# The first feature groups of a fused recurrence and two-layer network, taken unit by unit

## The chip, the cores and the metric

The kernel runs on one core of one Trainium2 chip. The metric is the time of one execution on the device, in microseconds (us). Engines: TensorE (PE, with its weight loads as PEld), VectorE (DVE), ScalarE (ACT), GpSimd (POOL) and SyncE (SP), which issues most DMAs; POOL issues the weights' loads.

## The reference

Four sequences of 768 steps with 8 heads of 48 dimensions go through a linear recurrence, and its output (3072 tokens of 384) through two networks:

```python
for t in range(S):
    cur = einsum('bhd,bhe->bhde', u * k[t], v[t])
    y[t] = einsum('bhd,bhde->bhe', r[t], state + cur)
    state = w[t][:, :, :, None] * state + einsum('bhd,bhe->bhde', k[t], v[t])
x = y.transpose(0, 2, 1, 3).reshape(B * S, H * D)
x = ((x @ w_a) * (x @ w_b)) @ w_out
h = x @ w_in
out = (maximum(h, 0) + alpha * minimum(h, 0)) @ w_out2
```

The first network has 1536 features, the second 2048. All data are float32.

## The kernel before, in words

**Products.** Each float32 operand of a large product is split in two: a high part (rounded to the type float32r) and a low part, the rest. A product is then three: high by high, low by high, high by low (`gemm3`, nine matmuls over three slices of 128, and `out1`, `out2` for the second factor). ACT makes the high part and DVE the low part.

**The recurrence.** It is cut into 12 units of 256 tokens. A unit has two forms of its inputs: `T` (transposed r, k, w; 112 partitions) and `N` (natural r, k, w). On `N`, DVE computes products of near pairs of steps (`natural`), which go through DRAM (`diag`: one store `mb`, eight loads into the diagonal blocks of the mask matrix `M`). On `T`, DVE runs a tree over distances 1 to 32 (`tree`); before each tree step at or above the unit's sub-block size, PE multiplies the far pairs (`level`, PSUM tile `psl`) and ACT copies them into `M` (`extract`; in unit 1 DVE does it for the second head of each pair). Then come the transposes of k (`ktrans`, `psk`, copied to `kn`), the state products (`dstate`, `psd`), the state (`state`) and the output (`yout`, `psx`), which ACT and DVE split into the high and low part of x. Each pair of units is a block of 512 tokens.

**The first network.** `mlp1` runs once per block over 12 groups of 128 features (`f`). A group has two products `pa` and `pb` (nine matmuls of 512 columns each), ACT's copy `ca` of pa, DVE's product `mul`, the split into `g`, and nine matmuls into three accumulators `acc`. At the block's end ACT copies the three results (`cp`), and POOL stores them to DRAM (`x2d`). The second network, `mlp2`, follows for all six blocks.

**Weights.** `load_w` brings each 128 x 384 weight as 64-bit floats and converts it: `sign`, `expo` and `low` on ACT, `join` on DVE, `hi` on ACT, `lo` on DVE. The order in block 0 is a, b, out of group 0, then of group 1, and so on. The loads stand on POOL; each load but the first six waits, through a small copy `tick`, for the weight six places earlier. All 36 weights of the first network stay in tiles of one pool (`w`, 37 tiles of 3072 bytes per partition); A0, N1 and V1 of the first units borrow five of them at the start.

**Pools.** PSUM has three pools that matter here: `psacc` (three banks: the accumulators, and at the start the levels of units 0 and 1), `psatt` (three banks: everything else of the recurrence) and `psh` (two banks: pa and pb). A tile of a pool is given out in the order in which tasks were added, except in `ws` and `psacc`, where whoever is ready takes one. `T` is a pool of one tile, so the next unit's T can be loaded when all readers of the last one are done. T of unit 1 has a tile of its own.

**The order of the work.** Nothing is scheduled by hand. The class `Tasks` (line 35) collects tasks with an engine, an estimated duration, a priority (lower goes first), the names they read and write, and a pool. `run` (line 94) plays them through: each engine takes the ready task with the lowest priority number. The instructions are then written out in the order found, so each engine's queue is fixed before the kernel runs. Between 4.5 us and the start of the first pa (planner's time), PE gets filler matmuls on the identity (`warm`) where it is idle or its recent work is thin.

```python
bank(lev):  "acc", "psacc"  if u < len(BLOCKS[0]) and lev  else  "att", "psatt"
NW = 37;  WL = 6;  pools: ws 3, x2 2, T 1, psatt 3, psh 2, psacc 3
K.fill += [first_pa[0], 2900]
```

Of the kernel before, what the change touches and what calls it, by code (L numbers as in the profile page):

```python
# [22 lines left out]
CH = 128  # L23
# [11 lines left out]
class Tasks:  # L35
# [58 lines left out]
    def run(self):  # L94
# [51 lines left out]

        while left:
            progress = True
            while progress:
                progress = False  # L150
                for eng, q in ready.items():
# [3 lines left out]
                    for k, (p, i) in enumerate(q):  # L155
                        if at[i] > now + 1e-9:
                            continue
                        if eng == "PE" and warming() and low(now + t[i][1], self.work.get(i, 0.0)):
                            filler()
                            progress = True  # L160
                            break
# [22 lines left out]
                        heapq.heappush(ev, (end, serial, i))  # L184
                        progress = True
# [6 lines left out]
            if i >= 0:  # L192
                left -= 1
                for h in users.get(i, ()):
# [17 lines left out]
def rwkv_then_moe_kernel(  # L212
# [53 lines left out]
    W = {}  # L266
    prev = []
    WL = int(6)

    def load_w(key, src, pr, after=()):  # L270
        behind = None
        prev.append(key)
        gate = len(prev) == 1
        if gate:
            after = list(after) + ["m1/d2"]
        if len(prev) > WL:
            behind = prev[-1 - WL]
            after = list(after) + [f"w{behind[0]}{behind[1]}"]
        nm = f"w{key[0]}{key[1]}"
        raw, ws = nm + "r", nm + "s"  # L280
        c = {}

        def ld():
            c["raw"] = wp.tile([128, 384, 2], U32, tag="w", name="raw", bufs=NW)
            if gate:
                nc.gpsimd.tensor_copy(tick, first_m[1][96:97, 0, 0, 32:33])
            if behind:

                nc.gpsimd.tensor_copy(tick, W[behind][0:1, 0, 0:1].bitcast(F32))
            nc.gpsimd.dma_start(out=c["raw"].bitcast(I64).rearrange("p n one -> p (n one)"), in_=src)  # L290

        def sign():

            c["s"] = xp.tile([128, 384], U32, tag="ws", name="ws", bufs=3)
            nc.scalar.activation(  # L295
                out=c["s"].bitcast(F16).rearrange("p (n b) -> p n b", b=2)[:, :, 1], in_=c["raw"][:, :, 1].bitcast(F32),
                func=ACTF.Copy, scale=2.0 ** -100)

        def low():

            nc.scalar.activation(
                out=c["s"].bitcast(U16).rearrange("p (n b) -> p n b", b=2)[:, :, 0], in_=c["raw"][:, :, 0],
                func=ACTF.Copy, scale=7.49 * 2.0 ** -32)

        def expo():
            h = c["raw"][:, :, 1].bitcast(F32)
            nc.scalar.activation(out=h, in_=h, func=ACTF.Copy, scale=2.0 ** -112)

        def join():
            nc.vector.scalar_tensor_tensor(  # L310
                out=c["s"], in0=c["raw"][:, :, 1], scalar=3, in1=c["s"],
                op0=ALU.logical_shift_left, op1=ALU.bitwise_or)

        def hi():
            W[key] = wp.tile([128, 2, 384], F32R, tag="w", name="w", bufs=NW)
            nc.scalar.copy(W[key][:, 0], c["s"].bitcast(F32))  # L316

        def lo():
            tt(W[key][:, 1], c["s"].bitcast(F32), W[key][:, 0].bitcast(F32), ALU.subtract)

        add("Pool", 1.1, pr - 40, ld, r=after, w=[raw], alloc=("w", raw), nbytes=128 * 3072)
        yield
        add("ACT", act(384), pr, sign, r=[raw], w=[ws, raw + "/h"], alloc=("ws", ws))
        add("ACT", act(384), pr, expo, r=[raw], w=[raw + "/h"])
        add("ACT", act(384), pr, low, r=[raw, ws], w=[ws])
        add("DVE", dve(384), pr, join, r=[raw + "/h", ws], w=[ws])
        add("ACT", act(384), pr, hi, r=[ws], w=[nm], alloc=("w", nm))
        add("DVE", dve(384), pr, lo, r=[ws, nm], w=[nm + "/l"])


# [5 lines left out]
    def unit(u, pr):  # L336
# [3 lines left out]
        T, V = f"T{u}", f"V{u}" if u != 1 else "V1/x"  # L340

        N = {y: f"N{u}/{y}" if u != 1 else f"N1{y}/x" for y in "rkw"}
# [11 lines left out]
        def bank(lev):  # L354

            if u < len(BLOCKS[0]) and lev:
# [17 lines left out]
        def zn(cc, hd, k):  # L374
            return f"Z{cc}{hd}{k}" if u else f"z{cc}{hd}/{k}"
# [29 lines left out]
        def new_t():  # L405
            cur["T", u] = ap_.tile([112, 3, 8, CH], F32, tag="T", name="T")
# [5 lines left out]
        if u != 1:  # L412
            add("HOST", 0, p0, new_t, w=[f"{T}/new"], alloc=("T", T))
# [365 lines left out]
    def mlp1(j, pr, xnames, us):  # L779
# [7 lines left out]
        def out1(f, ks, ms=(0, 1, 2)):  # L787
            if f == 0 and ks[0] == 0:
                c["acc"] = [pp.tile([128, n], F32, tag="acc", name=f"acc{m}", bufs=3) for m in range(3)]
            order = [(i, m) for i in ks for m in ms]  # L790
            for i, m in order:
                wi, gi = ((0, 0), (1, 0), (0, 1))[i]
                mm(c["acc"][m], W["o", f][:, wi, 128 * m:128 * m + 128], c["g", f][:, gi],
                   f == 0 and i == 0, f == F1 - 1 and i == 2)

        def add_out(f, p):
            g, wo = f"g{j}_{f}", f"wo{f}"
            if f == 0:
                for m in range(3):
                    add("PE", 0, p, lambda: None, r=[g + "/h"], w=[f"{acc}_{m}"], alloc=("psacc", f"{acc}_{m}"))  # L800
            if f == F1 - 1:
                for m in range(3):
                    add("PE", 3 * MM, p, lambda m=m: out1(f, (0, 1, 2), (m,)), r=[g + "/h", g + "/l", wo, wo + "/l"],
                        w=[f"{acc}_{m}"])
# [374 lines left out]
```

## Time and profile before

| | us |
|---|---|
| three runs | 1004.85, 1007.99, 1011.61 |
| median | 1007.99 |
| profiled execution, own time | 1009.12 |
| its span (first to last instruction) | 1007.3 |
| mean granted TensorE clock | 0.993 of full speed |

The busy times in the profile's rows are those of the one profiled execution, counted from the start of its span. A clock of 1.00 is TensorE's level of 2.4 GHz, 0.50 the one of 1.2 GHz; values between are means over a stretch. In a timeline row the bracket at the end gives the idle time of the engine before the first instruction and what ended it.

### The profile page before, as it was taken

What the parts mean: (1) busy time and instruction counts of PE and PEld (TensorE: products, weight loads), DVE (VectorE), ACT (ScalarE), POOL (GpSimd) and SP (SyncE); (2) the same over time, 40 slices, a digit from 0 to 9 for tenths busy, and PEclk for the clock granted to TensorE, in tenths of its full rate; (3) what the DMA queues carried; (4) which work ended last, traced back from release to release, by engine and by line L of the source; (5) the groups of instructions that cost most, each with busy time, mean ns of one, the idle gap of its engine ahead of it and who ended that gap; (6) DMA issues with size and microseconds to landing.
All of it is one profiled execution on the core that took longest, in us unless ns stands there. A gap on an engine that the chain in (4) does not pass through costs nothing.

```text
span 1007.3 us, 21086 instructions
## 1 busy us (share of the span) xinstructions
PE 978.8 (97%) x8800; PEld 823.5 (82%) x8800; DVE 728.4 (72%) x1215; ACT 431.3 (43%) x931; POOL 87.7 (9%) x173
## 2 busy tenths in 40 slices
PE   6899999999999999999999999999999999999998
PEld 3558787877788878878788888898989898999998
DVE  8979899899999979897935668555554645554643
ACT  0796987535444363534438994121211121211111
POOL 1324120100100010000004331000000000000000
PEclk9999999999999999999999999999999999999999
DMA  7895563324141441415116551010100100000000
GB/s 215 211 242 167 180 165 105 107 71 129 50 132 44 116 138 41 127 41 155 18 43 206 172 171 64 1 32 32 32 32 1 32 32 1 32 1 1 32 1 32
DMA packets 78158, 85.61 MB, mean 85 GB/s; under 512 B 55600, under 2 KB 64944, under 8 KB 76784
## 3 DMA queue, kind: packets, MB, share of 16 engines
q1 hardware_dynamic: 70896, 52.81, 19.7%
q0 software_dynamic: 7168, 31.46, 9.9%
q8 instruction: 69, 1.13, 0.5%
q14 instruction: 25, 0.20, 0.1%
HBM read 73.24 MB, written 11.01 MB: 84 GB/s over the span
## 4 chain that ended last, share of the span: by engine, by line
PE 61%; DVE 20%; DMA 8%; ACT 7%; issue 3%; SPq 1%; DVEq 0%; ACTq 0%
PE acd L768 15%; PE hb L768 15%; PE hp L768 10%; PE pb L768 6%; DMA T<-in_rkw_t_dram 6%; PE pa L768 6%; PE acc L768 6%; DVE T L257 5%; DVE e L257 4%; DVE A L483 4%; PE psl L564 2%; DVE a L257 2%; DVE N L257 2%; DVE g L257 2%; ACT ws L295 1%
## 5 line engine op out<-in xcount | busy, mean ns | idle before, releaser
L768 PE MATMUL acd<-w,g 128*128 128x384 f32 x864 | 192.6, 335 | 0.0
L950 ACT CAST g<-g 128x512 fp32r<-128x512 f32 x96 | 59.6, 621 | 281.7 <-PE hb L768 173.1
L768 PE MATMUL acc<-g,w 128*128 128x512 f32 x648 | 174.7, 399 | 1.1 <-ACT g L830 1.1
L768 PE MATMUL pa<-x,w 128*128 128x512 f32 x648 | 162.0, 395 | 0.6 <-ACT a L819 0.3
L768 PE MATMUL pb<-x,w 128*128 128x512 f32 x648 | 159.8, 391 | 0.6 <-ACT w L316 0.5
L768 PEld LDWEIGHTS acd<-w,g 128*128 128x128 f32 x864 | 154.2, 188 | 1.8
L768 PEld LDWEIGHTS pa<-x,w 128*128 128x128 f32 x648 | 121.7, 189 | 27.8 <-ACT x L719 1.1
L768 PEld LDWEIGHTS pb<-x,w 128*128 128x128 f32 x648 | 121.2, 188 | 27.0 <-ACT w L316 0.9
L768 PEld LDWEIGHTS acc<-g,w 128*128 128x128 f32 x648 | 118.7, 189 | 26.3 <-ACT g L830 1.7
L257 DVE TENSOR_TENSOR T<-T 112x1024 f32<-112x1024 f32 (+4 forms) x144 | 116.4, 809 | 20.8 <-DMA T<-in_rkw_t_dram 17.2
L257 DVE TENSOR_TENSOR g<-g,g 128x512 fp32r<-128x512 f32 x96 | 66.2, 690 | 81.9 <-ACT g L950 81.3
L768 PE MATMUL hp<-x,w 128*128 128x512 f32 x432 | 103.0, 391 | 0.0
L830 ACT CAST g<-a 128x512 fp32r<-128x512 f32 x72 | 44.4, 617 | 135.8 <-DVE a L257 134.5
L768 PE MATMUL hb<-x,w 128*128 128x512 f32 x432 | 102.0, 389 | 0.0
L768 PEld LDWEIGHTS hb<-x,w 128*128 128x128 f32 x432 | 81.1, 188 | 16.8
L768 PEld LDWEIGHTS hp<-x,w 128*128 128x128 f32 x432 | 80.8, 188 | 16.0
L768 PE MATMUL hb<-w,g 128*128 128x384 f32 x288 | 92.5, 335 | 0.0
L483 DVE TENSOR_REDUCE A<-e 128x16 f32<-128x768 f32 (+15 forms) x148 | 85.9, 580 | 2.0
L941 DVE TENSOR_SCALAR g<-hp,al 128x512 f32<-128x512 f32 x48 | 36.0, 751 | 63.0 <-PE hp L768 63.0
L257 DVE TENSOR_TENSOR a<-a,pb 128x512 f32<-128x512 f32 x72 | 49.1, 682 | 19.3 <-PE pb L768 18.5
L564 PEld LDWEIGHTS psl<-T 48*16 48x16 f32 (+4 forms) x2432 | 39.6, 107 | 23.0 <-issue 12.7
L819 ACT COPY a<-pa 128x512 f32<-128x512 f32 x72 | 41.9, 581 | 31.6 <-PE pa L768 31.2
(76 smaller groups left out, 1095.4 us busy)
## 6 DMA issues: line engine op xcount, KB each, us to landing
raw<-in_wt_dram POOLq DMA_DIRECT2D x68, 384.0 KB, 4.0
T<-in_rkw_t_dram SPq DMA_DIRECT2D x36, 448.0 KB, 6.3
N<-in_rkw_n_dram SPq DMA_DIRECT2D x10, 1152.0 KB, 8.3
x2d<-x POOLq DMA_DIRECT2D x36, 128.0 KB, 2.1
x2r<-x2d SPq DMA_DIRECT2D x36, 128.0 KB, 2.2
out_dram<-o SPq DMA_DIRECT2D x24, 192.0 KB, 1.9
V<-in_v_s_dram SPq DMA_DIRECT2D x11, 384.0 KB, 7.1
Z<-in_v_s_dram SPq DMA_DIRECT2D x44, 96.0 KB, 3.0
```

The source lines that it names most:

```text
L257: nc.vector.tensor_tensor(out=out, in0=a, in1=b, op=op)
L295: nc.scalar.activation(out=c["s"].bitcast(F16).rearrange("p (n b) -> p n b", b=2)[:, :, 1], in_=c["raw"][:, :, 1].bitcast(F32), func=ACTF. ...
L483: nc.vector.tensor_reduce(out=v[:, :, d:d + (n - 1) * (SUB + 1) + 1:SUB + 1], in_=part(st["e"], 0, n), axis=AX.X, op=ALU.add)
L564: nc.tensor.matmul(out=st["ps"][o0:o0 + ms, cc, q, zc * i:zc * i + zc], lhsT=t[b0:b0 + 48, 1, q0 + q, t0:t0 + ms], rhs=r[b0:b0 + 48, q0 + ...
L768: nc.tensor.matmul(out=out, lhsT=lhsT, rhs=rhs, start=start, stop=stop)
L819: nc.scalar.copy(c["a", f], c["pa"])
L830: nc.scalar.copy(c["g", f][:, 0], c["a", f])
L941: nc.vector.tensor_scalar(out=st["m", f], in0=st["h", f], scalar1=0.0, scalar2=al[:, f:f + 1], op0=ALU.min, op1=ALU.mult)
L950: nc.scalar.copy(st["g", f][:, 0], st["m", f])
```

## The change

In block 0 the first three feature groups are computed for each unit apart: first with the 256 columns of unit 0, all three groups, then with those of unit 1. pa and pb of such a half share one PSUM tile, `hx`, with pa in the first 256 columns and pb in the others. From the fourth group on all is as before, and the fillers end with that group's pa. So that the accumulators can be taken early, only unit 0's levels use `psacc`; those of unit 1 go to `psatt`. Weights are loaded and converted two at a time, in 19 tiles of twice the size, three pairs ahead; a pair's conversion is the same six operations with 768 columns. T is one lasting tile `Tp`, whose parts r, k and w are tracked by name from unit to unit. The tiles borrowed at the start are three larger ones; two of unit 0's four Z tiles move into the one of A0. The copies `x2` of a block's result use the `ws` tiles (in the last block, M). In the planner's first 75 us, ACT and DVE stay free for up to 0.5 us where a task of clearly lower priority number is about to become ready (`soon`).

```diff
+        ends = {}
+
+        def soon(eng, p, dur):
+            c, at_ = {}, {}
+            for i, end in ends.items():
+                for s in succ[i]:
+                    if t[s][0] == eng and t[s][2] < p - 4.0:
+                        c[s] = c.get(s, 0) + 1
+                        at_[s] = max(at_.get(s, 0.0), end + (self.LAT[t[i][0]] if t[i][0] != eng else self.SAME.get(eng, 0.0)))
+            return any(c[s] == need[s] and at_[s] < now + min(0.5, dur) for s in c)
...
+                        if now < 75.0 and eng in ("ACT", "DVE") and soon(eng, p, t[i][1]):
                             break
...
+    Tp = ap_.tile([112, 3, 8, CH], F32, name="Tp")
...
-    NW = 37
+    NW = 19
-    for tag, n in (("w", NW), ("ws", 3), ("x2", 2), ("x", 2), ("a", 2), ("g2", 2), ("psatt", 3), ("psh", 2), ("psacc", 3),
-                   ("e", 1), ("kn", 1), ("T", 1), ("N", 1), ("V", 1)):
+    for tag, n in (("w", NW), ("ws", 2), ("x", 2), ("a", 2), ("g2", 2), ("psatt", 3), ("psh", 2), ("psacc", 3),
+                   ("e", 1), ("kn", 1), ("N", 1), ("V", 1)):
...
-    WL = int(6)
+    WL = int(3)
...
-            c["raw"] = wp.tile([128, 384, 2], U32, tag="w", name="raw", bufs=NW)
+            c["raw"] = wp.tile([128, 2, 384, 2], U32, tag="w", name="raw", bufs=NW)
...
+            if i >= WL:
+                nc.gpsimd.tensor_copy(tick, W[prev[i - WL][0]][0:1, 0, 0:1].bitcast(F32))
+            nc.gpsimd.dma_start(out=c["raw"].bitcast(I64).rearrange("p x n one -> p x (n one)"),
+                                in_=src.rearrange("x p n -> p x n"))
...
+        add("Pool", 1.1, pr - 40, ld, r=after, w=[R], alloc=("w", R), nbytes=128 * 6144)
         yield
+        add("ACT", act(768), pr, sign, r=[R], w=[S_, R + "/h"], alloc=("ws", S_))
+        add("ACT", act(768), pr, expo, r=[R], w=[R + "/h"])
+        add("ACT", act(768), pr, low, r=[R, S_], w=[S_])
+        add("DVE", dve(768), pr, join, r=[R + "/h", S_], w=[S_])
+        add("ACT", act(768), pr, hi, r=[S_], w=[nm + "/h"], alloc=("w", nm))
+        add("DVE", dve(768), pr, lo, r=[S_, nm + "/h"], w=[nm + "/l"])
...
-        T, V = f"T{u}", f"V{u}" if u != 1 else "V1/x"
+        T, V = "T1" if u == 1 else "Tp", f"V{u}" if u != 1 else "N1b/v"
...
-            if u < len(BLOCKS[0]) and lev:
+            if u == 0 and lev:
                 return "acc", "psacc"
             return "att", "psatt"
...
-    def mlp1(j, pr, xnames, us):
+    def mlp1(j, pr, xnames, us, pre=0):
...
+            def product(k, i):
+                if h is None:
+                    c[k, f, h] = pp.tile([128, n], F32, tag="h", name="p" + k, bufs=2)
+                else:
+                    if "hx" not in c:
+                        c["hx"] = pp.tile([128, 512], F32, tag="h", name="ph", bufs=2)
+                    c[k, f, h] = c["hx"][:, 256 * i:256 * i + 256]
+                gemm3(c[k, f, h], W[k, f], X[blk][:, :, :, c0 + cs.start:c0 + cs.stop])
...
+            add("PE", 9 * t, p, lambda: product("a", 0), r=wn(("a", f)) + xr, w=[pa],
+                alloc=("psh", pa) if h is None else None, work=work)
+            add("ACT", act(m, True), p - 50, ca, r=[pa], w=[a], alloc=("a", a))
+            add("PE", 9 * t, p, lambda: product("b", 1), r=wn(("b", f)) + xr, w=[pb],
+                alloc=("psh", pb) if h is None else None, work=work)
+            add("DVE", dve(m), p - 50, mul, r=[pb, a], w=[a])
...
+        if pre:
+            add("HOST", 0, 0, lambda: None, w=["hx/a", "hx/b"], alloc=("psh", "hx"))
+        for h in range(2):
+            for f in range(pre):
+                p = pr(f + 0.5 * h)
+                step(f, p, h)
+                if f:
+                    add_out(f - 1, p, h)
+            if pre:
+                add_out(pre - 1, p, h)
-        for f in range(F1):
+        for f in range(pre, F1):
...
-                c["x2", m] = xp.tile([128, n], F32, tag="x2", name="x2", bufs=2)
+                c["x2", m] = M.rearrange("p a b c d -> p (a b c d)")[:, 512 * m:512 * m + n] if blk == len(BLOCKS) - 1 else xp.tile([128, 2, 384], F32, tag="ws", name="x2", bufs=2).rearrange("p x n -> p (x n)")[:, 0:n]
...
-            mlp1(j, lambda f, s=start[j], d=d: s + d * f, xn, BLOCKS[j])
+            mlp1(j, lambda f, s=start[j], d=d: s + d * f, xn, BLOCKS[j], 3 if j == 0 else 0)
```

## Rows read from the trace of the kernel before

**Rows 1.** Page, part 1: busy us (share of the span) and instructions of each engine.
```profile
PE 978.8 (97%) x8800; PEld 823.5 (82%) x8800; DVE 728.4 (72%) x1215; ACT 431.3 (43%) x931; POOL 87.7 (9%) x173
```

**Rows 2.** Busy time by stretch: length, engines with instructions, clock, DMA share, GB/s.
```profile
50.00:70.00 20.00, 17.54 (x320) 10.50 (x320) 14.24 (x29) 17.60 (x41) 6.31 (x12) 0.91 0.92 254
70.00:176.00 106.00, 101.66 (x1188) 82.07 (x1188) 96.20 (x166) 86.84 (x198) 23.40 (x42) 0.98 0.58 158
176.00:262.00 86.00, 84.02 (x1092) 68.25 (x1092) 79.45 (x140) 39.55 (x93) 3.23 (x6) 1.00 0.34 93
262.00:357.00 95.00, 92.08 (x1244) 75.10 (x1243) 88.79 (x153) 40.88 (x96) 3.21 (x6) 0.98 0.33 88
```

**Rows 3.** Timeline, PE, a filler run: start us, us, engine, line, output.
```profile
59.61 2.84 PE L1016 MATMUL warm<-idt 128*128 128x512 f32 x6
```

**Rows 4.** Chain of waits in order of time: start us, us, what.
```profile
45.83 5.01 DMA mb<-A
...
55.55 5.30 DMA M<-mb
...
69.81 2.37 PE pa L768 x9
...
170.54 2.04 PE pa L768 x9
...
622.75 1.58 PE acd L768 x9
```

**Rows 5.** Timeline, DVE and ACT: x of unit 0, of unit 1; copy of pa.
```profile
51.33 0.56 DVE L257 TENSOR_TENSOR x<-psx,x 128x384 fp32r<-128x384 f32 x1 [1.00 <-ACT x L719]
...
69.31 0.45 ACT L719 CAST x<-psx 128x384 fp32r<-128x384 f32 x1
...
74.50 0.56 ACT L819 COPY a<-pa 128x512 f32<-128x512 f32 x1
```

**Rows 6.** Timeline, weights: high part of b1, low parts of a2 and o2.
```profile
52.59 0.49 ACT L316 CAST w<-ws 128x384 fp32r<-128x384 f32 x1
...
63.41 0.56 DVE L257 TENSOR_TENSOR w<-ws,w 128x384 fp32r<-128x384 f32 x1
...
68.51 0.55 DVE L257 TENSOR_TENSOR w<-ws,w 128x384 fp32r<-128x384 f32 x1
```

**Rows 7.** Timeline, unit 1: transposes, state product, two extractions, output.
```profile
55.95 0.93 PE L610 MATMUL psk<-idt,T 112*128 112x112 f32 x8
...
58.54 1.14 PE L634 MATMUL psd<-v,kn 64*48 64x48 f32 x64
...
61.20 0.85 ACT L582 COPY M<-psl 8x128 f32<-8x128 f32 x4 [0.96 <-DVE M L580]
...
63.88 0.57 ACT L582 COPY M<-psl 32x512 f32<-32x512 f32 x1
...
64.56 2.22 PE L709 MATMUL psx<-M,Z 128*32 128x64 f32 x128 [2.10 <-issue]
```

**Rows 8.** ACT's groups by shape, whole span: count, busy us, mean ns, idle.
```profile
L830 ACT CAST g<-a 128x512 fp32r<-128x512 f32 x72 | 44.4, 617 | 135.8 <-DVE a L257 134.5 <-PE acc L768 1.3
...
L600 ACT COPY M<-T 48x1024 f32<-48x1024 f32 x21 | 22.0, 1047 | 6.3 <-DVE T L257 6.1
```

**Rows 9.** Page, part 5: DVE's tree on T; busy, mean, idle and releaser.
```profile
L257 DVE TENSOR_TENSOR T<-T 112x1024 f32<-112x1024 f32 (+4 forms) x144 | 116.4, 809 | 20.8 <-DMA T<-in_rkw_t_dram 17.2
```

**Rows 10.** Timeline at the end of block 1: PE, ACT, PE.
```profile
258.15 4.43 PE L768 MATMUL acc<-g,w 128*128 128x512 f32 x18
...
259.12 0.85 ACT L719 CAST x<-psx 128x384 fp32r<-128x384 f32 x2
...
264.28 1.21 PE L564 MATMUL psl<-T 48*16 48x16 f32 x128 [1.70 <-DVE T L257]
```

**Rows 11.** Timeline, PE: pa of the fourth feature group in block 0.
```profile
90.16 2.21 PE L768 MATMUL pa<-x,w 128*128 128x512 f32 x9
```

More of the change, by code (lines that the diff above doesn't have):

```diff
@@ L184, in run @@
                         heapq.heappush(ev, (end, serial, i))
+                        ends[i] = end
                         progress = True
@@ L785, in mlp1, with cols, accs, out1 @@
         MM = 0.2155 if n == 512 else 0.118
-        def out1(f, ks, ms=(0, 1, 2)):
-            if f == 0 and ks[0] == 0:
+        def cols(h):
+            return slice(0, n) if h is None else slice(256 * h, 256 * h + 256)
+        def accs(h, ms=(0, 1, 2)):
+            return [f"{acc}_{m}/{z}" for m in ms for z in ((0, 1) if h is None else (h,))]
+        def out1(f, ks, ms=(0, 1, 2), h=None):
+            if f == 0 and ks[0] == 0 and not h:
                 c["acc"] = [pp.tile([128, n], F32, tag="acc", name=f"acc{m}", bufs=3) for m in range(3)]
@@ L792, in out1, with names @@
                 wi, gi = ((0, 0), (1, 0), (0, 1))[i]
[L793 to L798, printed above, removed]
+                mm(c["acc"][m][:, cols(h)], W["o", f][:, wi, 128 * m:128 * m + 128], c["g", f, h][:, gi, cols(h)],
+                   f == 0 and i == 0 and not h, f == F1 - 1 and i == 2)
+        def names(f, h):
+            return f"{j}_{f}" if h is None else f"{j}_{f}h{h}"
@@ L799, in add_out @@
+        def add_out(f, p, h=None):
+            g, wo = "g" + names(f, h), wn(("o", f))
+            t = MM if h is None else 0.118
+            work = {} if h is None else {"work": 256 * 3}
+            if f == 0 and not h:
                 for m in range(3):
-                    add("PE", 0, p, lambda: None, r=[g + "/h"], w=[f"{acc}_{m}"], alloc=("psacc", f"{acc}_{m}"))
+                    add("PE", 0, p, lambda: None, r=[g + "/h"], w=accs(None, (m,)), alloc=("psacc", f"{acc}_{m}"))
             if f == F1 - 1:
@@ new lines, in add_out, with step @@
+            add("PE", 3 * t, p, lambda: out1(f, (2,), h=h), r=[g + "/l", wo[0]], w=accs(h),
+                work=256 * 3 if h is not None else 0)
+        def step(f, p, h=None):
+            a, g = "a" + names(f, h), "g" + names(f, h)
+            pa, pb = ("pa" + names(f, h), "pb" + names(f, h)) if h is None else ("hx/a", "hx/b")
+            cs = cols(h)
+            m = n if h is None else 256
+            t = MM if h is None else 0.118
+            work = 0 if h is None else 256 * 9
+            xr = xnames if h is None else xnames[4 * h:4 * h + 4]
+            def product(k, i):
[6 more added lines that the diff above has]
+                gemm3(c[k, f, h], W[k, f], X[blk][:, :, :, c0 + cs.start:c0 + cs.stop])
+            def ca():
+                c["as", f, h] = xp.tile([128, n], F32, tag="a", name="a", bufs=2)
+                nc.scalar.copy(c["as", f, h][:, cs], c["a", f, h])
@@ L1035, in first @@
             for cc in range(2):
-                for hd in range(2):
-                    first_z[cc, hd] = xp.tile([128, 8, 64], F32, tag=("x2", "a")[hd], name="z", bufs=2)
+                first_z[cc, 1] = xp.tile([128, 8, 64], F32, tag="a", name="z", bufs=2)
         for hd in range(2):
@@ L1083, in weights @@
                     next(gens[i - n], None)
-        weights((load_w((nm, f), wt1[f, i], start[0] + (start[1] - start[0]) / F1 * f - wlead + i)
-                 for f in range(F1) for i, nm in enumerate("abo")), WL - 1)
+        wf = wt1.rearrange("f x p n -> (f x) p n")
+        weights((load_w([("abo"[y % 3], y // 3) for y in (x, x + 1)], wf[x:x + 2],
+                        start[0] + (start[1] - start[0]) / F1 * (x // 3) - wlead + x % 3)
+                 for x in range(0, 3 * F1, 2)), WL - 1)
         for j in range(NB):
```

142 lines of the change are left out of this document (65 added, 77 removed).

## The prediction, made before the changed kernel ran

> **What bounds the kernel now.** I read the busy shares first [rows 1]: TensorE (PE) is busy 97% of the span, VectorE (DVE) 72%, ScalarE (ACT) 43%. A share over the whole span mixes stages, so the stretches come next [rows 2]. From 70 to 357 us PE is idle only 4.3, 2.0 and 2.9 us per block of the first layer, while DVE is busy 91 to 93%: two engines are close to being the limit there. Before 70 us the picture is another: PE shows 17.5 of 20 us busy between 50 and 70, but the timeline says with what. The rows called "warm" are matmuls on the identity that compute nothing of the result [rows 3]. So the first 70 us are work of units 0 and 1, with a PE that has little of its own to do.
>
> The chain of waits shows what these 70 us wait for [rows 4]: unit 1's score matrix leaves at 45.83, and the eight copies that bring its diagonal blocks back land at 60.85 (55.55 + 5.30). Behind them come extraction, state, output and the split of x. The first product of the first layer starts at 69.81, and it needs x of both units, although x of unit 0 was complete at 51.89 [rows 5]. After 69.81 the chain is almost all PE. So the end lies at 69.81 plus what PE has left then: whatever PE work moves ahead of that moment is gained, as long as x of units 2 to 11 still comes in time.
>
> **The change part by part.** The sum is made against the profiled execution's own 1009.12 us (span 1007.3), 1.1 us above the median of the runs, 1007.99.
>
> *Three feature groups by unit.* Nine 512-column matmuls follow each other in 2.04 us, 0.2267 each; nine of 384 columns take 1.58, 0.1756 each [rows 4]. The line through both puts 256 columns at 0.1245 (an estimate). Three groups are 81 matmuls: 18.36 us as now, 2 x 81 x 0.1245 = 20.2 us as halves. Unit 0's half, 10.1 us, may run between 51.9 and 69.8, where PE now runs fillers. What is left after x of unit 1 is 10.1 instead of 18.36: a gain of 8.3 us, if that half is finished by then.
>
> Its weights must be there. In the trace b1 got its high part at 53.08 (52.59 + 0.49), a2 its low part at 63.97, o2 at 69.06 [rows 6]. So groups 0 and 1 fit, the two products of group 2 just fit, and the output product of group 2 (nine matmuls, 1.1 us) probably does not: +1.1.
>
> *One PSUM bank for both products.* The halves write pa and pb into two column ranges of a single 512-column tile. The trace shows how this program treats one PSUM tile under two engines: at 61.20 ACT, idle for 0.96 us, begins its four copies out of a psl tile when DVE's copy out of that tile is done, although the two read other partitions [rows 7]. So I expect pb of a half to wait for ACT's copy of pa, and the planner's task list does not know of that wait. The hand-over is short: ACT's last extraction ends at 64.45 and psx starts at 64.56. A copy of 256 columns is about 0.40 us: 512 take 0.617 and 1024 take 1.047, so 0.84 ns per column [rows 8]. With 0.1 on either side that is 0.6 us. But ACT is in order: the copy of the first pa began at 74.50, 2.3 us after pa had ended at 72.18 [rows 4, 5]. The cost per half group lies between 0 (no such order) and 2.9 us; I take 1.0, nearer the undisturbed copy. Behind the waiting pb on PE stand the output product and unit 2's levels, and who waits for those is DVE's tree. In unit 1's half the waits are exposed: 3 x 1.0 = +3.0, bounds 0 and 8.7. In unit 0's half they stand under the wait for x of unit 1.
> The Trainium skill, "PSUM — Partial Sum Buffer", section "PSUM bank collisions raise a hardware error", says that two engines must not touch one bank in the same quarter of partitions at once, even in different columns, and that accesses have to be guarded by bank. The 0.96 us wait above agrees. By it the waits are there; if accesses to different columns ran free, the 3.0 would go.
>
> *Unit 1's levels move to the three-bank pool that its K transposes, state products and outputs use.* Now the transposes ran at 55.95 and the state product at 58.54, under the wait for the diagonal blocks [rows 7]. After the change three level tiles hold the three banks until extracted, so these two steps come behind the extraction: two transposes with their copies and the product, 55.95 to 59.68 now, 3.7 us, of which the extraction of the later levels hides about 1.0: +2.7. Against it, ACT ran weight operations before the second x of unit 1: psx ended at 66.78, that copy began at 69.31 [rows 5, 7], so up to 2.2 us can come back, since before 75 us the new planner holds ACT and DVE up to 0.5 us for a more urgent task. I take +0.5 for x of unit 1, bounds -3 and +6.
>
> *Weights in pairs.* One ACT operation of 768 columns takes the place of two of 384, four times per pair. Through 512 at 0.617 and 1024 at 1.047 us a 768-column cast is 0.83, two of 384 are 1.01 [rows 8]; as neighbours overlap by 0.1, some 0.1 us is saved per operation, 18 pairs x 4 x 0.1 = 7 us of ACT in block 0, where ACT is 82% busy [rows 2]. PE hides it: I count nothing. If the cover went, it would be a gain. The first pair lands later by one 384 KB transfer; behind the waiting ACT stand unit 0's copies, and x of unit 0 has 18 us in hand. POOL issues half as many loads and waits otherwise; its ticks keep the same lead of six weights. x2 sharing the weights' tiles can hold a conversion for the length of a store at the block ends; PE's 73 us in block 5 cover that.
>
> *One lasting tile T.* The loads of the next unit now wait for their own part of T instead of all of it. DVE stood 17.2 us in nine waits for those loads [rows 9]; the last readers of the parts end within some 2 us of each other, so at best 2 us per wait. SP issues them in order, with N and V behind. This helps DVE, not PE: nothing in the sum, bounds 0 and -3.
>
> *Sum.* -8.3 + 1.1 + 3.0 + 0.5 = -3.7: 1005.4 against the profiled execution, 1004.3 as a median.
>
> What is late next: x of units 4 and 5. Its last copy ends at 259.97, and block 1's last output products run from 258.15 to 262.58; then PE already waits 1.70 us for the tree of the unit after [rows 10]. There are 2.6 us in hand, less than the 3.7 gained, so about a microsecond must come from the attention side; the T waits can give it.
>
> **The rivals.**
> *The whole head start holds and the chain before it shortens.* The held ACT and DVE bring x of unit 1 forward by 3 us, pb doesn't wait, the T waits halve. For it: ACT's 2.5 us between psx and the second x [rows 5, 7]. Against: the single bank. -8.3 + 1.1 - 3 and some -1 of idle time: 1009.1 - 11.2 = 997.9, 996.8 as a median.
> *The head start is given back at the first block boundary.* If x of units 4 and 5 comes when it comes now, PE stops after 2.6 us gained, whatever it had, and a second wait like the 1.70 us one comes on top [rows 10]: 1009.1 - 2.6 + 1.7 = 1008.2, 1007.1 as a median. For it: DVE's 92% there. Against: its waits for T.
> *Slower: unit 1 stands behind unit 0's halves.* The half groups ahead of unit 1's transposes and state product on PE's in-order queue each hold it while pb waits for an ACT that is late as at 74.50: 3 x 2.6 = 7.8, plus the 2.7 from the banks: x of unit 1 10.5 us later. Net -8.3 + 1.1 + 3.0 + 10.5 = +6.3: 1014.3 as a median. It decides from x of unit 1 later than about 74 us. For it: ACT 88% busy from 50 to 70 [rows 2]. Against: PE has gaps, and only what is planned before unit 1's steps holds them.
>
> **How the numbers follow.** Forecast 0.48, whole head start 0.22, given back 0.18, slower rival 0.12. The range must reach the first rival with its scatter and the slower one's near end: 994 to 1014. Below 997.9 (faster by over 1%, about what a measurement of this kernel can tell from no change; its three runs span 1004.85 to 1011.61): two thirds of the first rival and a twentieth of the forecast, 0.17. Above 1018.1: a third of the slower rival and little else, 0.05. Within 1%: 0.78.
>
> **What would show it.** Right: 256-column products on PE from about 52 us, fewer warm rows between 52 and 70, pb idle behind ACT's copy of pa, the first full-width product (the fourth group) some 4 us before its 90.16 of now [rows 11], the copy of block 0's first result earlier by as much, and block 1 ending near 259. Wrong: x of unit 1 after 74, or weights of group 2 after it; x of units 4 and 5 not earlier, with PE idle before block 2; or pb starting while ACT still reads pa, which takes the 3.0 out.

## The result and the profile after

The changed kernel took 1017.08 us (median of 6 runs, 1015.46 to 1026.42) beside 1007.47 for the kernel before: a ratio of 1.0106, interval 1.0081 to 1.0131. It is slower by about 1%, where 1004.3 with a range of 994 to 1014 had been forecast. The execution profiled below took 1020.28 us (span 1018.3).

The busy time by stretch, with the columns of [rows 2]:

```profile
50.00:70.00 20.00, 15.33 (x201) 12.87 (x197) 14.23 (x26) 14.45 (x27) 2.75 (x5) 0.91 0.85 258
70.00:176.00 106.00, 99.13 (x1396) 81.01 (x1397) 93.70 (x143) 83.21 (x150) 16.84 (x22) 0.98 0.55 155
176.00:262.00 86.00, 84.24 (x990) 68.50 (x992) 79.04 (x138) 37.77 (x88) 3.26 (x6) 1.00 0.33 90
```

Between 50 and 70 us, where the half groups of unit 0 were to fill PE, PE is busy 15.33 us, less than the 17.54 of before with its fillers. From 70 to 176 it is idle 6.9 us instead of 4.3. The PE timeline shows the first half product where it was expected, and then a long wait. Between the half groups stand unit 1's transposes (psk), state product (psd) and outputs (psx):

```profile
51.43 1.63 PE L789 MATMUL ph<-x,w 128*128 128x256 f32 x9
...
56.29 3.86 PE L789 MATMUL ph<-x,w 128*128 128x256 f32 x18 [0.25 <-ACT a L863]
...
62.23 2.42 PE L789 MATMUL ph<-x,w 128*128 128x256 f32 x18
...
65.28 0.96 PE L631 MATMUL psk<-idt,T 112*128 112x112 f32 x8
...
69.89 2.29 PE L789 MATMUL ph<-x,w 128*128 128x256 f32 x9 [3.29 <-ACT a L863]
...
74.21 1.14 PE L655 MATMUL psd<-n,kn 64*48 64x48 f32 x64
...
77.55 2.14 PE L730 MATMUL psx<-M,Z 128*32 128x64 f32 x128
...
95.60 2.23 PE L789 MATMUL pa<-x,w 128*128 128x512 f32 x9
```

The last row is the first full-width product: 95.60 us, against 90.16 [rows 11]. ACT's timeline shows why 69.89 came so late:

```profile
60.04 0.75 ACT L603 COPY M<-psl 16x256 f32<-16x256 f32 x2
...
66.12 1.07 ACT L316 ACTIVATE ws<-raw 128x768 f16<-128x768 f32 x1 [2.83 <-DMA raw<-in_wt_dram]
67.06 0.55 ACT L603 COPY M<-psl 32x512 f32<-32x512 f32 x1
...
69.48 0.36 ACT L863 COPY a<-ph 128x256 f32<-128x256 f32 x1
...
71.03 0.53 ACT L636 COPY kn<-psk 128x448 f32<-128x448 f32 x1
...
72.33 0.53 ACT L636 COPY kn<-psk 128x448 f32<-128x448 f32 x1
...
79.77 0.48 ACT L740 CAST x<-psx 128x384 fp32r<-128x384 f32 x1 [0.57 <-PE psx L730]
```

ACT stood 2.83 us before the conversion of a pair whose load had not landed. Behind it in its queue stood unit 1's last extraction (its psl had been done at 62.29, 60.94 + 1.35 by PE's timeline) and the copy of pa. ACT begins its last copy of x of unit 1 at 79.77, against 69.31 [rows 5]: 10.5 us later.

Only a part of the 10.5 us is that load. The last extraction begins 3.2 us later (67.06 against 63.88 in [rows 7]). From there to the start of unit 1's outputs on PE it was 0.7 us before (63.88 to 64.56) and is 10.5 now (67.06 to 77.55): 9.8 more. From the outputs to the copy of x it is 2.2 us instead of 4.8: 2.5 less. Before, transposes and state product were done at 59.68, ahead of the extraction; now, with three banks for all of unit 1, they come behind the extraction of its earlier levels, among half groups on PE and weights on ACT. The chain of waits runs through the late load, and then through the fillers that stand in PE's queue before the state product and the outputs:

```profile
45.57 6.86 DMA raw<-in_wt_dram
...
55.24 10.78 DMA raw<-in_wt_dram
...
73.42 0.86 PE warm L1071 x2
...
75.90 1.72 PE warm L1071 x4
```

DVE's waits for the loads of T are no shorter in the change: the last number, 17.8 us, answers to 17.2 in [rows 9]. In e11 below, the kernel before with the lasting T alone, it is 8.4; the rows of the two pages:

```profile
L273 DVE TENSOR_TENSOR Tp<-Tp 112x1024 f32<-112x1024 f32 (+2 forms) x132 | 106.7, 808 | 19.5 <-DMA Tp<-in_rkw_t_dram 17.8
...
L258 DVE TENSOR_TENSOR Tp<-Tp 112x1024 f32<-112x1024 f32 (+2 forms) x132 | 107.0, 811 | 13.0 <-DMA Tp<-in_rkw_t_dram 8.4
```

By milestones, after against before: fourth group's pa +5.4; first copy of block 0's result 179.73 against 175.34 (+4.4); third copy of block 1's 271.71 against 269.91 (+1.8), of block 2's 366.35 against 364.32 (+2.0), of block 3's 458.56 against 454.02 (+4.5); first output product of the second network 633.59 against 622.58 (+11.0); span +11.0. So what block 0 lost is in large part made up by the end of block 1, and most of the 11.0 us of this execution is lost after 366 us. PE's timeline, the change first, then the kernel before:

```profile
401.61 0.24 PE L585 MATMUL psl<-Tp 48*16 48x16 f32 x3 [2.20 <-issue]
...
403.23 4.04 PE L789 MATMUL pa<-x,w 128*128 128x512 f32 x9
...
493.95 1.21 PE L585 MATMUL psl<-Tp 48*16 48x16 f32 x128 [2.34 <-DVE Tp L273]
...
562.37 1.20 PE L789 MATMUL acc<-g,w 128*128 128x512 f32 x4 [1.01 <-ACT x L909]
...
607.60 2.34 PE L789 MATMUL pa<-x,w 128*128 128x512 f32 x9 [0.81 <-ACT a L863]
...
633.59 1.83 PE L789 MATMUL acd<-w,g 128*128 128x384 f32 x9 [0.29 <-ACT M L909]
```

```profile
486.36 1.30 PE L564 MATMUL psl<-T 48*16 48x16 f32 x128 [0.84 <-DVE T L257]
...
622.58 1.75 PE L768 MATMUL acd<-w,g 128*128 128x384 f32 x9
```

The wait of 2.20 us before 401.61 lies in a run of psl products, and nothing in the profile explains it; the nine matmuls of pa behind it took 4.04 us, where nine took 2.21 in [rows 11]. This may be of this execution alone, the second longest of the six. The last three waits are not: all six profiled kernels with pairs and the lasting T (the change, e1, e2, e4, e8, e15) have them with the same 1.0, 0.8 and 0.3 us, and none of the others has any in that stretch. ACT's timeline shows the first of them:

```profile
561.00 0.83 ACT L338 CAST w<-ws 128x768 fp32r<-128x768 f32 x1 [5.10 <-PE pb L789]
561.74 0.58 ACT L909 COPY x<-acc 128x512 f32<-128x512 f32 x1
```

The third copy of block 4's result, done by PE at 544.58, stood in ACT's queue behind a pair's conversion that waited 5.10 us, and PE waited for the bank that the copy frees. Why pairs and lasting T together give this order was not tried.

### The profile page after: what moved, and what is told of

It is laid out like the page before. It is cut to its first block, busy times and chain, and to the rows that moved or that the text cites. A ratio compares the mean times of both kernels' runs of the same rounds, so it can differ in the third digit from the quotient of the medians.

```text
span 1018.3 us, 20902 instructions
## 1 busy us (share of the span) xinstructions
PE 982.9 (97%) x8879; PEld 829.0 (81%) x8879; DVE 724.1 (71%) x1153; ACT 422.7 (42%) x801; POOL 69.3 (7%) x108
## 4 chain that ended last, share of the span: by engine, by line
PE 59%; DVE 19%; ACT 11%; DMA 7%; issue 3%; POOL 0%; SPq 0%; ACTq 0%; DVEq 0%; POOLq 0%
PE acd L789 15%; PE hb L789 14%; PE hp L789 9%; PE pa L789 6%; PE pb L789 6%; PE acc L789 5%; DVE Tp L273 4%; DVE e L273 4%; DMA Tp<-in_rkw_t_dram 3%; DVE A L504 3%; DMA raw<-in_wt_dram 3%; ACT ws L316 2%; PE psl L585 2%; DVE g L273 2%; ACT ws L322 2%
## 5 line engine op out<-in xcount | busy, mean ns | idle before, releaser
L789 PE MATMUL acc<-g,w 128*128 128x512 f32 (+1 forms) x675 | 176.3, 390 | 2.7 <-ACT x L909 1.0
L789 PE MATMUL pa<-x,w 128*128 128x512 f32 x621 | 156.1, 396 | 2.0 <-ACT a L863 1.3
L789 PE MATMUL pb<-x,w 128*128 128x512 f32 x621 | 154.6, 393 | 1.8 <-DVE a L273 1.8
L789 PEld LDWEIGHTS acc<-g,w 128*128 128x128 f32 x675 | 121.9, 190 | 26.8 <-ACT x L909 1.4
L789 PEld LDWEIGHTS pa<-x,w 128*128 128x128 f32 x621 | 116.7, 190 | 29.4 <-ACT a L863 2.7
L789 PEld LDWEIGHTS pb<-x,w 128*128 128x128 f32 x621 | 115.6, 188 | 27.6 <-issue 1.8
L273 DVE TENSOR_TENSOR Tp<-Tp 112x1024 f32<-112x1024 f32 (+2 forms) x132 | 106.7, 808 | 19.5 <-DMA Tp<-in_rkw_t_dram 17.8
L871 ACT CAST g<-a 128x512 fp32r<-128x512 f32 (+1 forms) x75 | 44.9, 599 | 132.9 <-DVE a L273 129.3
L273 DVE TENSOR_TENSOR a<-a,pb 128x512 f32<-128x512 f32 x69 | 46.9, 680 | 25.2 <-PE pb L789 21.9
L273 DVE TENSOR_TENSOR g<-a,g 128x512 fp32r<-128x512 f32 (+1 forms) x75 | 49.8, 663 | 15.2 <-ACT g L871 14.9
```

The lines of the kernel that those rows point to most:

```text
L273: nc.vector.tensor_tensor(out=out, in0=a, in1=b, op=op)
L789: nc.tensor.matmul(out=out, lhsT=lhsT, rhs=rhs, start=start, stop=stop)
L871: nc.scalar.copy(c["g", f, h][:, 0, cs], c["as", f, h][:, cs])
```

## The experiments

Ratios are to the kernel before, measured in the same session. Theory A: ACT's in-order queue is held by pairs of weights, and x of unit 1 comes late. B: the half groups on PE, with their one bank, make it late. C: the three banks of unit 1 do. D: the held engines or the lasting tile lose time later. S: the planner's order was a good draw, and any edit costs several us.

**A pair held back (e1).** Theory A's own remedy: the three pairs from the sixth on are converted only after x of unit 1.

```diff
-        add("ACT", act(768), pr, sign, r=[R], w=[S_, R + "/h"], alloc=("ws", S_))
+        add("ACT", act(768), pr, sign, r=[R] + (["x0/11h"] if 5 <= i < 8 else []), w=[S_, R + "/h"], alloc=("ws", S_))
```

> Edit: in the planner alone, the conversion of the sixth to eighth pair of weights (from b3 with out3 on) may begin only when the second x of unit 1 has been copied. Theory A (ACT's in-order queue is held by the load of a pair that nobody needs yet): the last extraction of unit 1 moves from 67.1 to about 63, x of unit 1 from 80 to 73 (+-1.5), the first full-width product from 95.6 to 89, and the time falls by 5 to 8 us to 1009 to 1012. Rival B (the half groups on PE and their one bank hold unit 1): x of unit 1 stays after 78 and the time within 2 us of 1017. Rival C (three banks for all of unit 1): x of unit 1 stays after 76.

1013.73 us, 1.0075 (1.005 to 1.010). The extraction came at 65.85 instead of 67.06, but x of unit 1 at 79.69: ACT's copies of unit 1's transposes ran at 70.82 and 71.98, hardly before the change's 71.03 and 72.33. The time is 3.4 us less than the change's, with intervals that overlap. x of unit 1 after 76 is what theory C expected; the load that theory A named was one place of several.

**Parts taken out (e2, e3).** e2: the change without half groups, with unit 1's levels in their old bank (`3 if j == 0 else 0` becomes 0). e3: pairs and the tiles that go with them, without half groups, held engines and lasting T.

> Edit: all feature groups full width as before, unit 1's levels back in the accumulators' banks; pairs, lasting T and the held engines stay. Theory A: the load of a pair still stands in ACT's queue before x of unit 1, so x of unit 1 comes 3 to 6 us later than the 69.8 of before and there is no head start: 1010 to 1014. Rival B: x of unit 1 at 70 or earlier and the time at 1004 to 1008. Rival C: as B.

> Edit: the pairs of weights with their tiles (and x2 in them) are all that is left of the change: no halves, old banks, T by unit, engines not held. Theory A: ACT waits for 768 KB loads before x of unit 1; x of unit 1 at 72 to 76, time 1010 to 1014. Rivals B and C: 1005 to 1009, and less ACT time in block 0 than before.

e2: 1026.85, 1.0203 (1.0171 to 1.0235), above every range set for it, with x of unit 1 at 76.89. e3: 1013.95, 1.0074 (1.0046 to 1.0102). So the pairs alone, which I had counted at nothing, cost 7.4 us, with x of unit 1 at 78.64; B and C are not needed for that. In e3 DVE's 768-wide join stood ahead of unit 1's last corrections, which left at 48.74 (45.83 in [rows 4]).

**The planner told of the bank (e4).** pa and pb of a half get one name, so that pb is planned behind ACT's copy of pa.

```diff
-            pa, pb = ("pa" + names(f, h), "pb" + names(f, h)) if h is None else ("hx/a", "hx/b")
+            pa, pb = ("pa" + names(f, h), "pb" + names(f, h)) if h is None else ("hx/a", "hx/a")
```

> Edit: the two halves of the shared bank get one name, so the planner knows that pb waits for the copy of pa and the next pa for the product with pb; the instructions are the same in another order. Rival B: the waits of PE behind ACT's copy (0.25 and 3.29 us) go to other work, x of unit 1 3 us or more earlier, time 1010 to 1014. Theory A: the last extraction still stands behind the sixth pair's load, x of unit 1 at 77 to 80, time within 2.5 us of 1017.

1020.58, 1.0143 (1.0115 to 1.0172): not better. That the planner doesn't know of the wait is not the loss. Nor is the late extraction by itself: here the last one began at 62.01, 5 us before the change's, and x of unit 1 still came at 80.22, with the copies of its transposes at 70.49 and 71.64.

**Singles again, and the combinations (e5 to e8).** e5: the whole change with the loads and conversions of before. e6: half groups alone. e7: pairs and half groups. e8: the change without held engines (`if now < 75.0` becomes `if now < 0.0`).

> The whole change except that weights come singly again (one 384 KB load, four 384-wide ScalarE operations and two VectorE operations a weight, 37 buffers, six loads ahead, x2 in its own two buffers). Theory A (the pairs make x of unit 1 late: their 768-wide operations and their later landing stand in front of unit 1's copies on ScalarE): x of unit 1 comes back from 79.8 to 69 to 73 us, the first full-width product from 95.6 to 84 to 90, and the time to 998 to 1004. Rival B (half groups on TensorE with their one bank make it late): x of unit 1 stays at 76 to 80 us and the time at 1010 to 1018. Rival D (the held engines and the lasting tile lose it later): x of unit 1 comes back, but the block boundaries fall behind again and the time is 1007 to 1015.

> The half groups alone: the kernel before with the first three groups of block 0 by unit and the three-bank pool for unit 1; single weights, no held engines, T by unit. Theory A: the head start is what the prediction's first term says (8.3 us at most, less 3 for the one bank): x of unit 1 at 69 to 73 us, time 998 to 1004. Rival B: x of unit 1 later than 75 us and 1007 to 1014. Rival D: as theory A, and 3 us or more faster than the singles with held engines and lasting tile.

> Pairs and half groups, without held engines and without the lasting tile. Theory A: x of unit 1 at 77 to 80 us as with pairs alone (78.6), the half groups give back some 5 us of that: 1007 to 1011. Rival D (held engines or lasting tile cost the rest of the loss): the same, 1007 to 1011, where the full change has 1017. If neither of these two parts matters: 1014 to 1018.

> The whole change without the held engines. Rival D by its first half (an engine held for a task that is about to be ready moves later work back): 1008 to 1012. If the lasting tile alone is to blame, or neither: 1015 to 1019. Theory A by itself says nothing but that x of unit 1 stays at 77 us or later.

e5 1017.71, 1.009 (1.0059 to 1.012). e6 1014.42, 1.0076 (1.0045 to 1.0106). e7 1021.39, 1.0126 (1.0093 to 1.0159). e8 1019.06, 1.0106 (1.0079 to 1.0134). Theory A falls as the only cause: without pairs the change is as slow. Half groups alone (e6, with the three banks that go with them) cost 6.5 us (1014.42 less 1007.93), pairs alone 7.4, both together 13.5 (1021.39 less 1007.93), above both ranges set for e7. These two add; the parts in general don't: the whole change, with held engines and lasting T on top, costs 9.6, less than e7, and e2, the same without half groups, 20.3. The held engines make no difference that the whole change shows (1.0106 either way).

What theory C names is seen in the traces. From the end of ACT's last extraction of unit 1 to the start of its outputs on PE there are 0.10 to 0.35 us in all eleven kernels with unit 1's levels in the old bank, and 7.3 to 14.9 us in all nine with the three banks (9.9 in the change, 7.35 in e6). Banks and half groups were always put in and taken out together, so their shares stay open.

In e6, x of unit 1 is at 71.92 on ACT, and yet the first half product of unit 1 starts at 76.21. DVE's timeline of e6 shows what stood between:

```profile
71.55 0.56 DVE L272 TENSOR_TENSOR x<-psx,x 128x384 fp32r<-128x384 f32 x1
72.03 1.22 DVE L272 TENSOR_TENSOR T<-T 112x1024 f32<-112x1024 f32 x1
73.16 0.95 DVE L272 TENSOR_TENSOR e<-N,un 128x768 f32<-128x768 f32 x1
74.03 0.55 DVE L272 TENSOR_TENSOR x<-psx,x 128x384 fp32r<-128x384 f32 x1
```

and PE's timeline of e6 behind it:

```profile
73.34 1.95 PE L582 MATMUL psl<-T 48*60 48x32 f32 x64 [2.14 <-issue]
75.22 1.19 PE L786 MATMUL acc<-g,w 128*128 128x256 f32 x6
76.21 2.12 PE L786 MATMUL ph<-x,w 128*128 128x256 f32 x9
```

Two operations of unit 2 run on DVE before the second half of x, and PE's queue has unit 2's level, which needs them, ahead of the products that need x.

**An edit without work, and the tile alone (e9 to e11).** e9 and e10 change one number of the planner of before (`wlead = 20` to 19; `ahead = 20` to 19). e11 is the kernel before with the lasting T alone.

> The kernel before, every task and tile the same; one number of the planner changed: the lead of the weights' due times is 19 us instead of 20. Theory S (the order that the planner wrote before is one good draw, and any edit that makes it draw again costs several us, whatever it does): 1010 to 1018. Theories A and B (the parts of the change cost by what they do): 1005 to 1010, as before.

> The kernel before, every task and tile the same; the head start of the units' due times is 19 us instead of 20. Theory S: 1010 to 1018. Theories A and B: 1005 to 1010.

> The kernel before with the lasting tile for transposed operands alone. My sum had 0 to -3 us for it: 1004 to 1008. Theory S: 1010 to 1018, with the loss in stretches where no instruction waits for a load of this tile.

e9 1008.52, 1.0007 (0.9989 to 1.0026). e10 1004.75, 0.9975 (0.9956 to 0.9993). e11 1005.9, 0.9987 (0.9973 to 1.0001). Theory S falls in its wide form: of two redrawn orders one moved the time by +0.8 us and the other by -2.9, so it is not so that any edit costs several us. The 6.5 and 7.4 us are more than these two moved it, but each is also the price of one order, as e12 shows.

**Unit 2 put behind x of unit 1 (e12).** e6, with this on unit 2's tree from its second level on, and on its first natural product:

```diff
-            add("DVE", dve(8 * CH), p, halves, r=RK + Wn, w=RK)
+            add("DVE", dve(8 * CH), p, halves, r=RK + Wn + (["x0/11l"] if u == 2 and h > 1 else []), w=RK)
```

> The half groups alone (1014.4), and unit 2's tree from its second level on and its first natural product are made to wait for VectorE's half of x of unit 1, which they had been put in front of (it ran at 74.03 us, ScalarE's half at 71.92). If the late start of unit 1's half groups (76.2 us, the full-width products of before 69.8) is what eats the head start: they start at 72.5 to 74, the first full-width product comes at 86.5 to 88.5 instead of 90.6, and the time is 1010 to 1012.5. Theory S: the start comes forward but the time stays within 1012 to 1018, lost again later.

1010.75, 1.0037 (1.0021 to 1.0053): 3.7 us less than e6, though the two intervals overlap a little. PE's timeline of e12:

```profile
74.00 0.98 PE L786 MATMUL ph<-x,w 128*128 128x256 f32 x6 [0.53 <-ACT x L737]
75.59 1.69 PE L786 MATMUL ph<-x,w 128*128 128x256 f32 x12 [0.62 <-DVE x L272]
77.94 1.34 PE L786 MATMUL ph<-x,w 128*128 128x256 f32 x9 [0.66 <-ACT a L860]
```

The products now follow x directly, as expected; the first full-width product, at 89.76, did not come as early as the 86.5 to 88.5 expected. So a part of the 6.5 us is likely the order that the half groups brought, and not their work.

**Where the pairs lose (e13 to e15).** e13: e3, with the joins of the first three pairs behind unit 1's corrections. e14: also the fifth and sixth load behind the landed corrections (POOL's tick reads M first). e15: the whole change with both edits and e12's.

```diff
-        add("DVE", dve(768), pr, join, r=[R + "/h", S_], w=[S_])
+        add("DVE", dve(768), pr, join, r=[R + "/h", S_] + (["A16"] if i < 3 else []), w=[S_])
...
+            if i in (4, 5):
+                nc.gpsimd.tensor_copy(tick, M[96:97, 1, 0, 0, 32:33])
```

> Pairs alone (1013.95), and VectorE's joins of the first three pairs stand behind the last row sum of unit 1's corrections. With pairs alone the corrections left VectorE at 48.74 us (45.83 before), with a 768-wide join and a wait of 0.70 in front of them. If this is where the pairs start to be late: the corrections leave at 45 to 46, x of unit 1 comes at 75 to 76 instead of 78.6, and the time is 1010 to 1012. If the loads in flight and ScalarE's waits for them set it: x of unit 1 stays at 77 to 79 and the time at 1012 to 1016.

> As the run with the joins behind the corrections, and the loads of the fifth and sixth pair also wait until unit 1's corrections have landed in the masks M, so that fewer 768 KB loads run beside those small transfers. If the loads beside them made the masks late (the transfers took 6.3 and 5.8 us with pairs, 5.0 and 4.3 before): the first extraction of unit 1 on ScalarE at 61 to 63 us instead of 66.8, x of unit 1 at 70 to 73, and 1007 to 1010. If not: x of unit 1 as in the run without this, or later where the held loads come too late for the weights.

> The whole change (1017.1) with three orders mended: joins of the first three pairs behind unit 1's corrections, the fifth and sixth load behind the masks, unit 2's first tree and natural work on VectorE behind x of unit 1. If these orders are what the change loses by: x of unit 1 at 72 to 75 us instead of 79.8, the first full-width product at 88 to 91 instead of 95.6, 1006 to 1011. If the loss lies in the widths of the operations themselves or in the held engines: 1013 to 1018.

e13 1014.77, 1.0068 (1.005 to 1.0087). The corrections left at 45.98 and x of unit 1 came at 71.52 instead of 78.64, and the time did not move. So the late x of unit 1 is not, by itself, what the pairs cost. In e13 the fourth group starts at 92.31 and the seventh at 117.58, 25.3 us for three groups; before it was 90.16 to 112.20, 22.0. The waits of e13 from 84 to 182 us (in total, times, longest) show PE's output products waiting for ACT, and ACT for a buffer and for loads:

```profile
PE acc L790 <- ACT g L872: 5.5, 2, 3.0
...
ACT ws L315 <- DVE w L272: 5.0, 2, 4.7
...
ACT ws L315 <- DMA raw<-in_wt_dram: 3.5, 3, 1.5
```

The kernel before has 1.1, 2.1 and no such wait in that stretch. e14 1012.47, 1.0049 (1.0031 to 1.0068): unit 1's first extraction came at 54.12, x of unit 1 at 69.78, the time 2.3 us less than e13, with intervals that overlap, and not the 1007 to 1010 expected. e15 1024.88, 1.0164 (1.014 to 1.0188), the worst but one and above both ranges set for it, shows most plainly how a wait holds what stands behind it. ACT's extractions of unit 1 in e15:

```profile
56.74 0.75 ACT L607 COPY M<-psl 16x256 f32<-16x256 f32 x2
...
65.40 0.57 ACT L607 COPY M<-psl 32x512 f32<-32x512 f32 x1
```

Between them ACT waits 4.8 us in one piece for the load held back, which took 9.48 us to land. x of unit 1 came at 80.85. The remedy put the same wait in a worse place.

**Which property of the pairs (e17, e18).** e17: e3 with the six operations cut into two of 384 columns, the load and tiles of pairs kept. e18: e3 with two 384 KB loads into a pair's tile, the operations kept.

> Pairs alone (1013.95; the 768 KB load, a pair's tile, 19 of them, three pairs ahead), but each of the conversion's six operations is cut into two 384-wide ones with a release of their own, as before. If the pairs lose by the width of the operations (ScalarE and VectorE are held 1.07 and 0.95 us at a time, and a weight is ready only with its neighbour): 1007 to 1010.5. If they lose by the loads (768 KB land later, and a pair's first operation waits for both halves): 1012 to 1016.

> Pairs alone with two 384 KB loads into the pair's tile instead of one of 768 KB; the operations 768 wide. If the size of one load is the loss: 1007 to 1010.5. If the width of the operations or the gate by pairs is: 1012 to 1016.

e17 1015.08, 1.0083 (1.0052 to 1.0115); e18 1013.47, 1.0058 (1.0034 to 1.0081). Neither width nor size of load, taken back alone, gives the 7 us back. In e17 x of unit 1 stands at 69.66, as before, and the seventh group at 118.08. What e3, e13, e17 and e18 share is the count: two conversion buffers of double size where three stood, which x2 uses too, a weight ready only with its pair's buffer, and loads released two weights at a time. None of that was tried, and the cause of the pairs' 7 us stays open.

**A version under both (e16).** e11 with `ahead = 19`.

> The kernel before with the lasting tile and the units' due times 1 us later, the two edits that stood at 0.9987 and 0.9975: if they add, 1003 to 1005; if each is only another draw of the same order, 1004 to 1008.

1005.34, 0.998 (0.9963 to 0.9996). With e10's 0.9975 it is the only version under the kernel before whose interval ends below 1. That they add isn't shown: the product of the two ratios, 0.9962, lies just outside the interval.

## Why the prediction was wrong, point by point

- **What bounds the kernel.** Right in block 0: PE work moved ahead of x of unit 1 is taken off behind it. From x of unit 1 on ACT to the fourth group's pa the change needs 15.8 us (79.77 to 95.60), before 20.9 (69.31 to 90.16): 5.0 saved, where 8.3 - 1.1 - 3.0 = 4.2 was forecast. e12 has 16.3. But the end is not the first product plus what PE has left: the lag is 5.4 us at the fourth group, 1.8 at the end of block 1 and 11.0 at the end.
- **One bank.** The wait is there: pb began at 69.89, 0.05 us after ACT's copy of pa had ended at 69.84. The Trainium skill, "PSUM — Partial Sum Buffer", section "PSUM bank collisions raise a hardware error", has accesses guarded by bank even in different columns, and the trace agrees: the program waits so. (The 0.96 us wait in [rows 7] is between copies that read other partitions, so it is a wait by the whole bank, wider than the quarter of partitions that the prediction names with it.) But the term was over-sized: in unit 1's half PE's waits for that copy show 0 in the change and at most 0.66 (e12) in the other kernels with half groups, not 3.0. In unit 0's half it is 3.5 us in the change, and there unit 1's state product stood behind it.
- **x of unit 1, +0.5 with bounds of -3 and +6: the step that failed first.** It measured +10.5 us. The term for the banks was +2.7: transposes and state product behind the extraction, 3.7 us long with 1.0 hidden. Extraction to outputs grew by 9.8 instead. The 3.7 us are what these steps took in their old place; in the change the copies of the transposes stand on ACT behind weights and half groups, and the state product on PE behind a half group and fillers. Half groups with their banks give +2.6 on ACT (e6), and 6.4 for the first product that needs x (76.21 against 69.81); pairs alone, in the old bank, +9.3 (78.64), by a later extraction. I had not counted that ACT is 88% busy there [rows 2] and that what is added to its queue or DVE's before 70 us stands in front of something of unit 1.
- **"Weights in pairs ... PE hides it: I count nothing. ... the first pair lands later by one 384 KB transfer": the other step that failed.** Pairs alone cost 7.4 us. I looked for the cost in the first pair, with 18 us in hand for x of unit 0. In the change ACT waited for a later one, 10.78 us from issue to landing; but in the kernel before a single load issued at 58.9 took 9.51, and ACT shows no wait for a load from 50 to 70 us, so the length of a load alone is not what differs. In e13 PE waits 5.5 us in the middle of block 0 for an ACT that waits for buffers and loads. Which property of the pairs does it stays open. ACT's busy time did fall, from 431.3 us [rows 1] to 422.7, and it did not help.
- **"x2 sharing the weights' tiles ...; PE's 73 us in block 5 cover that".** Not in the change: PE waits 1.0, 0.8 and 0.3 us there, first of all for such a copy. I had looked for a conversion held by a store; here the copy stood behind a conversion.
- **Lasting T, 0 to -3.** Measured -1.8 alone (e11, interval -2.7 to +0.1 us). Its waits for T fell from 17.2 us to 8.4, and the time hardly moved, as "this helps DVE, not PE" had it. But they are 17.8 in the change, and 8.2 in e10, which has no lasting T, so how long they are goes with the order, and that the tile shortens them is not shown.
- **Held engines.** Counted as up to 2.2 us off x of unit 1; no difference in the change, and e2 against e3 shows 12.9 us more with held engines and lasting T where there are no half groups. Which of the two costs that was not tried.
- **The slower rival.** It had x of unit 1 10.5 us later and 1014.3; measured 10.5 and 1017.08. That its 10.5 came out to the tenth is luck, since its 7.8 from waiting pb's is not what the trace has; its mechanism is right in part: unit 1's state product, at 74.21, does stand behind a half group's pb, at 69.89, in PE's queue, but what held that pb was ACT waiting for a load. It was given 0.12.
- **The planner's order.** With parts that cost 13.5 us in e7 and 9.6 in the whole change, and repairs that make e15 worse, an edit's price on this kernel seems to be set by which queue entry lands ahead of which. The two neutral redraws moved the time by +0.8 and -2.9 us; a price below some 3 us can't be told from such a redraw here.

## What to carry to other kernels

An operation off the bounding engine is not free if it stands in an in-order queue: ask which load or buffer it waits for, and what stands behind it. Two conversion buffers of double size where three stood, and half as many loads, cost 7 us here though ACT's busy time fell; that the lost slack is the cause is a suspicion, not shown. A step moved behind another is not priced by its own length: transposes and state product took 3.7 us, and the stretch that they were moved into grew by 9.8. A delay at the start need not be the delay at the end: follow it from block to block before calling it the cause. Before pricing a head start, price the arrival of the thing it is ahead of, part by part; here two of the parts, each tried alone, would have shown a loss.

## What was not expected of the hardware

A PE left idle can pay twice. In e3 PE had 5.46 us of idle time ahead of unit 1's outputs, and its granted clock from 70 to 80 us is 0.66, a mean of the two levels, 1.2 and 2.4 GHz. The same 128 matmuls took 3.96 us there and 2.22 in [rows 7]. In the change the clock is 0.66 from 403 to 410 us, behind the wait of 2.20 us, and nine matmuls of 512 columns took 4.04 us instead of the 2.21 of [rows 11]. It is not so after each wait: behind the one of 2.34 us before 493.95 the clock stays at 1.00 (457 to 500 us). The stretch of e3, then its row on PE:

```profile
70.00:80.00 10.00, 7.26 (x135) 5.23 (x135) 4.33 (x6) 8.25 (x13) 1.24 (x3) 0.66 0.77 260
```

```profile
72.74 3.96 PE L731 MATMUL psx<-M,Z 128*32 128x64 f32 x128 [5.46 <-issue]
```

Over all executions of this study, within one kernel, a mean clock lower by 0.001 goes with a span longer by 0.83 us. The kernel before ran at 0.9948 (88 executions), the change at 0.9922 (6): some 2 of the 9.6 us between their medians by that slope, an estimate, and no proof that the clock is the cause, since idle time lengthens the span as well. The two profiled executions have the same mean clock, 0.993.

Small transfers beside large ones: from the last issue of the eight 16 KB copies of unit 1's corrections to their landing it took 5.3 us before [rows 4]. Over the eleven kernels with 768 KB loads it is 3.7 to 9.1 us (longest in e13), median 5.7; over the nine with 384 KB loads 2.8 to 5.3, median 4.1. The copies tend to land later beside the larger loads, but when the loads are issued moves as well, so that their size does it is not shown.
